# The first loads and statistics of a transformer block, in another order

## Chip, cores and metric

The kernel runs on one core of a Trainium2 chip. The metric is the device time of one execution in microseconds, the median of several runs. Before the change it is 292.81 us, the median of 3 runs (292.77 to 293.06).

## What is computed

A block with attention and an MLP over 2048 tokens of 640 features, bf16 in and out. Cut to what matters here:

```python
x = A_x                                           # 1 x 2048 x 640
h = x + attention(layernorm(x), wq, wk, wv, wo)   # 32 heads of 20, four segments of 512 tokens,
                                                  # causal softmax in a segment, linear memory between segments
out = h + silu(layernorm(h) @ w1) @ w2            # 640 -> 1728 -> 640

def layernorm(x):
    m, v = mean(x), var(x)                        # over the 640 features
    return (x - m) / sqrt(v + 1e-5)
```

The first segment's attention needs the normalized tokens of blocks 0 to 3 (128 tokens each), transposed so that features lie on partitions, and the weights wq, wk, wv (640 x 640, 800 KB each).

## The kernel before

The program is a list of named tasks. Each task issues a few instructions on one engine, and each engine runs its own instructions in the order in which the tasks stand in a hand-written list, `ORDER` (from line 382). No planner moves anything: a task that waits holds up everything behind it on its engine. In the list, a digit after the colon is the buffer or PSUM bank that the task takes, and a letter after a slash picks the engine where there is a choice (A is ScalarE, D is VectorE, G is GpSimd). `Tracker` (line 45) works out the semaphore waits from what each instruction reads and writes. One rule in it matters below: PSUM banks are one region each, and a read of PSUM by any engine other than TensorE is booked as if it were a write (lines 81 to 84), so that a later writer of the bank waits for that reader.

The work around the change is the beginning of the first segment. For token block b the tasks are:

- `x0`, `x1`, `x2`: loads of block 0, block 1, blocks 2 and 3 (line 595), all on SyncE's queue. Behind them on SyncE, in the list's order: the query weights in two pieces (`w_q0`, `w_q1`), the key weights in two pieces (`w_k0`, `w_k1`), the value weights (`w_wv`), `beta`, and then `x4` and `x8`, the tokens of blocks 4 to 11, which wait for the first key piece.
- `n1_stb`: mean and variance of block b. On VectorE that is two bn_stats, a bn_aggr, and for the blocks called early an addition of eps (lines 784 to 793). On ScalarE it is two activations over the 640 features that accumulate, the mean and then the squares (lines 778 and 780). Blocks 0, 1, 3 are on VectorE and block 2 on ScalarE; for that one a small task `n1_mnb` on ScalarE gives the mean in its final scale (line 801).
- `n1_rsb`: the power -1/2 on GpSimd; one instruction for early blocks (line 808), two for the others (lines 811 and 813).
- `n1_apb`: subtract the mean, multiply by the result, on VectorE (line 819).
- `n1_tpb`: five 128 x 128 transposes on TensorE as matmuls with the identity, into a pair of PSUM banks (line 828).
- `n1_teb`: copies these out of PSUM into `tT`, on ScalarE (line 837) or VectorE (line 838).
- `pr000x`, `pr001x`, `pr001y`, `pr000y`: the first projections of queries and keys from the raw weights, in halves of two blocks (line 752). x needs blocks 0 and 1, y needs blocks 2 and 3. Each is cut into `.0` (three chunks of 128 features) and `.1` (two chunks).
- `re_wqc`, `re_wkc`: copies of the weights into the arrangement that the later projections use (lines 745 and 747).

`zpad` is a small array of zeros that VectorE clears first. TensorE begins with matmuls on it that compute nothing (`fill25`, `fill4`, `fill8`, `fill2`, by their number, lines 636 to 638); `fill4`, `fill8` and `fill2` all write PSUM bank 5. `warm` is an activation on ScalarE that fetches the table of functions ahead of its first use (line 618). In the list of before, the order on TensorE is fill25, fill4, fill8, n1_tp0, n1_tp1, fill2, n1_tp3, pr000x.0, n1_tp2, pr000x.1, pr001x, pr001y, pr000y. Block 2's transpose takes banks 4 and 5.

After these come the rest of the segment, which alternates scores, exponentials, masks and products with values, and the other segments and the MLP woven between them.

Of the kernel before, what the change touches and what calls it, by code (L numbers as in the profile page):

```python
# [11 lines left out]
PE, AC, DV, PO, SP = "pe", "act", "dve", "pool", "sp"  # L12
# [333 lines left out]
D = 640  # L346
# [26 lines left out]
KS = [range(0, 3), range(3, 5)]  # L373
# [7 lines left out]

ORDER = """
x0:0 zpad:0 iota fill25:7 vpad0 x1:3 sel halfc mq0 x2:5,6 warm:0 w_q0:0 epsc w_q1 n1_st0:1 w_k0:0 w_k1 w_wv:0 n1_st1:0
n1_rs0 beta n1_ap0:0 n1_rs1 fill4:5 n1_st2:5,1 n1_st3:4 fill8:5 mq1 n1_tp0:2 n1_ap1:2 n1_rs3 n1_te0:1 n1_tp1:0 n1_rs2
fill2:5 n1_ap3:3 n1_mn2 n1_te1 n1_tp3:6 n1_ap2 re_wq1/A:0 pr000x.0:3 n1_te3/D x4:2,10,11,1 n1_tp2:4 pr000x.1
x8:9,8,4,7 n1_te2 pr001x.0:1 qe000x/D:0 re_wk1/G pr001x.1 re_wk2/A pr001y.0:2 re_wk4/G pr001y.1 qe001x pr000y.0:6
qe001y pr000y.1 re_wk3/G pr010.0/C:0 pa001:2 qe000y ex001:1 re_wq2/G qk0a0:4,1 lsc0 pr010.1 e0a2:0 lsc1 pr011.0:7
qe010/D:0 e0a0 pr011.1 qk0b0:0,2 qe011/D pr020.0/C:6 e0b2:3 mk0a pb001 pr020.1/C re_wk0/G n1_st4:3 e0b0 qk0e0:2,4
pr021.0:7 re_wq4/G e0e0:5 n1_st5:1 v00.0:0 vpad2 n1_rs4 e0e2 v00.1 qe020/D:0 pr021.1 n1_rs5 n1_st10:7 ve00:0 qk1a0:2,4
# [94 lines left out]
def build(nc, es, A_x, A_wq, A_wk, A_wv, A_wo, A_beta, B_x, B_w1, B_w2, out):  # L484
    T = Tracker()
# [9 lines left out]
    G = Graph(pools)  # L495
# [7 lines left out]
    wv_sb = sb("wv_sb", [128, NC, D], BF16)  # L503
# [65 lines left out]
    def R(*items):  # L569
        r = []  # L570
        for a, subs in items:
            r += a.keys(subs)
        return r

    def dma(name, reads, writes, fn, prio, bw, kind="plain", lane=None, engs=(SP,)):
        ln = T.lane(name) if lane is None else lane

        def emit(eng):
            T.add(eng, lambda e: fn(e), reads=R(*reads), writes=R(*writes), lane=ln)
        cost = {"tr": 1.31, "plain": 0.47, "sb": 0.72, "fix": 0.47}[kind]  # L580
        t = G.task(name, {e: cost for e in engs}, emit, reads, writes, prio, mode=kind, bw=bw)
        return t
# [4 lines left out]
    X = [G.alloc("x") for _ in range(12)]  # L587
    W = {k: G.alloc(k) for k in ("wq", "wk", "wv", "wo", "w1", "w2")}
    C = G.alloc("const")
# [3 lines left out]
    sT0 = G.alloc("sT")  # L593

    def load_x(b0, n, prio, bw=2.1, kind="plain", engs=(SP, AC)):
        s0 = b0 % 12
        dma(f"x{b0}", [(W["wk"], ["p"])] if b0 >= 4 else [], [(X[b], [0]) for b in range(b0, b0 + n)],
            lambda e: e.dma_start(out=x_tok[:, s0:s0 + n, :], in_=xv[:, b0:b0 + n, :]), prio, bw, kind, engs=engs)

    def load_w(k, dst, src, prio, bw, wr, kind="plain", engs=(SP, AC)):  # L600
        dma("w_" + k, [(W["wk"], ["p"])] if kind == "plain" else [], wr, lambda e: e.dma_start(out=dst, in_=src), prio, bw, kind, engs=engs)

    cw = lambda w: w.rearrange("(c p) e -> p c e", p=128)
    load_x(0, 1, -100, 2.30, "fix", (SP,))
    load_x(1, 1, -99, 2.33, "fix", (SP,))
    load_w("wv", wv_sb[:, :, :], cw(A_wv), -98, 4.96, [(W["wv"], [0])], "fix", (SP,))
    load_x(2, 2, -97, 4.79, "fix", (SP,))
    dma("beta", [], [(C, ["beta_bc"])],
        lambda e: e.dma_start(out=beta_bc[:, :],
                              in_=A_beta.rearrange("(o n) -> o n", o=1).to_broadcast([128, H])), -92, 4.65, "fix")  # L610
    for w_, (n_, src) in enumerate((("q", A_wq), ("k", A_wk))):
        for z, ks in enumerate(KS):
            k0_, k1_ = ks[0], ks[-1] + 1
            load_w(f"{n_}{z}", wraw[:, w_, k0_:k1_, :], cw(src)[:, k0_:k1_, :], -94 + w_, 6.58, [(sT0, [f"{n_}{z}"])] + ([(W["wk"], ["p"])] if n_ + str(z) == "k0" else []), "fix",
                   (SP,))
    G.task("zpad", {DV: 0.3}, lambda e_: T.add(DV, lambda e: e.memset(zpad[:, :], 0.0), writes=R((C, ["zpad"]))),
           [], [(C, ["zpad"])], -101)
    G.task("warm", {AC: 1.15}, lambda e_: T.add(AC, lambda e: e.activation(
        out=w2_sb[:, NF - 1:NF + 1, :], in_=zpad[:, 0:1].unsqueeze(2).to_broadcast([128, 2, D]), func=ACT.Tanh),
        reads=R((C, ["zpad"])), writes=R((W["w2"], [4, 5]))), [(C, ["zpad"])], [(W["w2"], [4, 5])], -100)  # L620
# [28 lines left out]
    def vpad(par, vt, wr=()):  # L649
# [8 lines left out]
        writes=["iota"], prio=-70)  # L658
    cst("sel", DV, 0.12, lambda e: e.tensor_scalar(out=ident[:, :], in0=iot[:, :], scalar1=0.0, scalar2=None,
                                                   op0=ALU.is_equal), reads=["iota"], writes=["sel"], prio=-70)  # L660
    sel = ident[:, :].rearrange("p (r e) -> p r e", e=32)[:, :, 0:VS]
# [5 lines left out]
        out=bsel[:, :], in_=bsel[:, :], pattern=[[0, NG], [-32, 4]], compare_op=ALU.is_equal, fill=0.0, base=-DH,  # L667
        channel_multiplier=1), reads=["bsel"], writes=["bsel"], prio=-1)
    cst("lsc2", DV, 0.25, lambda e: e.tensor_reduce(
        out=lsc[:, :], in_=bsel[:, :].rearrange("p (g r) -> p g r", r=4), axis=mybir.AxisListType.X, op=ALU.add),  # L670
# [95 lines left out]
    def layer_norm(tag, b, xa, xsub, dstA, i, prio):  # L766
# [5 lines left out]
        def e_stats(eng):  # L772
# [17 lines left out]
            if early:  # L790
                T.add(DV, lambda e: e.tensor_scalar(out=mvt[:, s, 1:2], in0=mvt[:, s, 1:2], scalar1=EPS, scalar2=None,
                                                    op0=ALU.add),
                      reads=R((st, ["mv"])), writes=R((st, ["mv"])))
        early = tag == "n1_" and b in (0, 1, 3)
        onact = tag == "n1_" and b == 2
        G.task(f"{tag}st{b}", {AC: 1.6} if onact else {DV: 1.03}, e_stats, [(xa, xsub)],
               [(st, ["s0", "mv"] if onact else ["s0", "s1", "mv"])] + ([(xn, [0])] if onact else []), prio)
        if onact:
# [55 lines left out]
    def declare_front(s):  # L854
# [5 lines left out]
        for i in range(4):  # L860
            layer_norm("n1_", 4 * s + i, X[4 * s + i], [0], xTa, i, k0 + P["ln1"] + P["ln1s"] * i if s else -30 + i)
# [531 lines left out]
```

## Time and profile before

| | |
|---|---|
| median of the runs | 292.81 us |
| the profiled execution | 292.8 us |
| its span, first to last instruction | 291.1 us |
| TensorE busy in the span | 283.0 us (97%) |
| ScalarE busy | 224.7 us (77%) |
| VectorE busy | 208.7 us (72%) |
| GpSimd busy | 138.1 us (47%) |
| granted TensorE clock | 1.00 throughout |

Times in the trace count from the first instruction. A row of a timeline has the start, the time to the end of the last of the merged instructions, the engine, the line of the kernel, the operation, what it writes and reads, how many, and in brackets how long the engine was idle before it and what ended that. A row of the chain of waits has start, length and the piece of work. Matmuls overlap, so the time of one says less than the distance between two.

### The profile page before, as it was taken

What the parts mean: (1) busy time and instruction counts of PE and PEld (TensorE: products, weight loads), DVE (VectorE), ACT (ScalarE), POOL (GpSimd) and SP (SyncE); (2) the same over time, 40 slices, a digit from 0 to 9 for tenths busy, and PEclk for the clock granted to TensorE, in tenths of its full rate; (3) what the DMA queues carried; (4) which work ended last, traced back from release to release, by engine and by line L of the source; (5) the groups of instructions that cost most, each with busy time, mean ns of one, the idle gap of its engine ahead of it and who ended that gap; (6) DMA issues with size and microseconds to landing.
All of it is one profiled execution on the core that took longest, in us unless ns stands there. A gap on an engine that the chain in (4) does not pass through costs nothing.

```text
span 291.1 us, 10526 instructions
## 1 busy us (share of the span) xinstructions
PE 283.0 (97%) x4587; PEld 156.9 (54%) x4587; DVE 208.7 (72%) x435; ACT 224.7 (77%) x286; POOL 138.1 (47%) x275
## 2 busy tenths in 40 slices
PE   8999989999999999999999999999999999999995
PEld 6544434445544446566643554655565557754674
DVE  5599889769998679369979972776676659436513
ACT  4999999999999999999689989999849750024300
POOL 4686668608670766609516761638435531200000
PEclk9999999999999999999999999999999999999999
DMA  7916439854565333343551327512110031340004
GB/s 207 350 57 125 85 65 303 116 55 79 121 110 126 67 86 101 47 76 60 101 183 17 66 43 102 78 19 49 25 25 2 2 69 26 75 131 0 3 5 160
DMA packets 48734, 24.86 MB, mean 85 GB/s; under 512 B 38896, under 2 KB 47472, under 8 KB 48688
## 3 DMA queue, kind: packets, MB, share of 16 engines
q1 hardware_dynamic: 48688, 24.19, 37.9%
q8 instruction: 36, 0.59, 0.9%
q14 instruction: 10, 0.08, 0.1%
HBM read 10.41 MB, written 2.62 MB: 45 GB/s over the span
## 4 chain that ended last, share of the span: by engine, by line
PE 79%; ACT 13%; DVE 4%; DMA 2%; POOL 1%; issue 1%; SPq 0%; DVEq 0%; ACTq 0%
PE ps_all L565 41%; PE ps_all L566 23%; ACT PT L1024 9%; PE ps_all L1003 7%; PE ps_all L1059 5%; ACT PT L1020 2%; DMA x_tok<-in_A_x_dram 2%; PE ps_all L1130 1%; PE ps_all L752 1%; PE ps_all L1268 1%; ACT ex L930 1%; POOL PT L1036 1%; DVE om L1149 1%; ACT oTs L1073 1%; PE ps_all L1189 1%
## 5 line engine op out<-in xcount | busy, mean ns | idle before, releaser
L1024 ACT ACTIVATE PT<-ps_all 128x1024 bf16<-128x1024 f32 x122 | 117.9, 1030 | 7.9 <-PE ps_all L1003 6.8
L1036 POOL TENSOR_SCALAR_AFFINE_SELECT PT<-PT 128x512 bf16<-128x512 bf16 x128 | 81.6, 666 | 71.6 <-ACT PT L1024 59.5
L1281 ACT ACTIVATE th<-ps_all 128x512 f32<-128x512 f32 (+1 forms) x56 | 31.5, 591 | 30.1 <-PE ps_all L565 22.5
L1287 DVE SCALAR_TENSOR_TENSOR sT<-th,ps_all 128x512 bf16<-128x512 f32 (+1 forms) x56 | 36.2, 661 | 16.8 <-ACT th L1281 16.5
L1020 ACT ACTIVATE PT<-ps_all 128x2048 bf16<-128x2048 f32 x19 | 35.7, 1878 | 3.5 <-PE ps_all L1003 3.4
L565 PE MATMUL ps_all<-w_sb,sT 128*128 128x320 bf16 x252 | 37.0, 299 | 0.0
L565 PE MATMUL ps_all<-tT,w_sb 128*128 128x512 bf16 x151 | 36.4, 380 | 0.0
L1324 DVE SCALAR_TENSOR_TENSOR x_tok<-ps_all,x_tok 128x640 bf16<-128x640 f32 (+1 forms) x17 | 13.2, 782 | 24.5 <-PE ps_all L566 16.1
L565 PEld LDWEIGHTS ps_all<-w_sb,sT 128*128 128x128 bf16 x252 | 23.7, 98 | 11.0 <-issue 1.7
L566 PE MATMUL ps_all<-w_sb,sT 128*32 128x320 bf16 x784 | 28.8, 299 | 0.0
L785 DVE BATCH_NORM_STATS2 stt<-x_tok 128x6 f32<-128x320 bf16 x62 | 27.0, 478 | 2.0 <-DMA x_tok<-in_A_x_dram 1.9
L566 PE MATMUL ps_all<-tT,w_sb 128*32 128x512 bf16 x436 | 27.1, 380 | 0.0
L566 PEld LDWEIGHTS ps_all<-w_sb,sT 128*32 128x32 bf16 x784 | 20.1, 97 | 6.7 <-issue 0.9
L565 PEld LDWEIGHTS ps_all<-tT,w_sb 128*128 128x128 bf16 x151 | 13.6, 98 | 16.1 <-issue 1.9
L1111 POOL TENSOR_TENSOR otok<-otok,om 128x320 bf16<-128x320 bf16 x24 | 18.2, 781 | 4.2 <-DVE otok L1098 4.2
L565 PE MATMUL ps_all<-wv_sb,tT 128*128 128x320 bf16 x130 | 19.9, 300 | 0.2 <-DVE zf L677 0.2
L811 POOL TENSOR_TENSOR rst<-mvt,eps_c 128x1 f32<-128x1 f32 x29 | 5.8, 201 | 27.4 <-DVE mvt L788 27.4
L819 DVE TENSOR_SCALAR xn_rot<-x_tok,mvt,rst 128x640 bf16<-128x640 bf16 x32 | 16.7, 533 | 2.5 <-POOL rst L813 1.3
L813 POOL TENSOR_TENSOR rst<-rst,eps_c 128x1 f32<-128x1 f32 x29 | 16.4, 567 | 2.3
L1246 DVE TENSOR_TENSOR x_tok<-ps_all,x_tok 128x640 bf16<-128x640 f32 x16 | 13.0, 812 | 6.0 <-PE ps_all L565 6.0
L1059 PE MATMUL ps_all<-PT,Vx 128*32 128x512 bf16 (+3 forms) x384 | 16.9, 300 | 0.2 <-ACT PT L1024 0.2
L1098 DVE TENSOR_TENSOR otok<-ps_all,rd 128x320 bf16<-128x320 f32 x32 | 15.7, 491 | 1.1
(116 smaller groups left out, 427.8 us busy)
## 6 DMA issues: line engine op xcount, KB each, us to landing
out_dram<-x_tok SPq DMA_DIRECT2D x15, 160.0 KB, 2.0
w_sb<-in_B_w_dram SPq DMA_DIRECT2D x5, 432.0 KB, 4.6
x_tok<-in_A_x_dram SPq DMA_DIRECT2D x3, 640.0 KB, 5.1
w_sb<-in_B_w_dram SPq DMA_DIRECT2D x3, 480.0 KB, 4.1
QKV<-QK SPq DMA_DIRECT2D x12, 72.0 KB
wv_sb<-in_A_wv_dram SPq DMA_DIRECT2D x1, 800.0 KB, 8.9
wo_sb<-in_A_wo_dram SPq DMA_DIRECT2D x1, 800.0 KB, 4.8
w_sb<-in_B_w_dram SPq DMA_DIRECT2D x1, 640.0 KB, 4.7
```

The costliest lines, as they stand in the source:

```text
L565: return [lambda e: e.matmul(out, lhsT=lhsT, rhs=rhs, start=start, stop=stop)]
L566: return [lambda e, p=p: e.matmul(out[p:p + 32, :], lhsT=lhsT[:, p:p + 32], rhs=rhs, start=start, stop=stop, tile_position=(0, p)) for p i ...
L785: T.add(DV, lambda e, hh=hh: e.bn_stats(out=stt[:, s, 6 * hh:6 * hh + 6], in_=xb[:, 320 * hh:320 * hh + 320]), reads=R((xa, xsub)), writes ...
L819: T.add(eng, lambda e: e.tensor_scalar(out=xn_rot[:, xn.slot, :], in0=x_tok[:, b % 12, :], scalar1=mvt[:, s, 0:1], scalar2=rst[:, s, :], o ...
L1003: fns.append(lambda e, j=j, o=o, r=r, q0=q0, q1=q1, qa=qa, ka=ka: e.matmul(ps_all[:, o:o + q1 - q0], lhsT=ka[32 * r:32 * r + DH, 128 * j:1 ...
L1020: T.add(AC, lambda e: e.activation(out=o, in_=src, func=ACT.Exp, scale=SCALE), reads=[("ps", z.slot + q) for z in (a, b) for q in range(2) ...
L1024: T.add(AC, lambda e: e.activation(out=pt[:, pta.slot, q0:q0 + 2, 0:width], in_=sc3[:, b0:b0 + 2, 0:width], func=ACT.Exp, scale=SCALE), re ...
L1036: fns.append(lambda e, v=v: e.affine_select(out=v, in_=v, pattern=[[0, 4], [1, 128]], compare_op=ALU.is_ge, fill=0.0, base=0, channel_mult ...
L1059: fns.append(lambda e, j=j, r=r, h=h, pa=pa, pt=pt, co=co, q0=q0, ji=ji: e.matmul(bank(po)[32 * r:32 * r + 32, q0:hi], lhsT=vtile(vx)[:, j ...
L1111: T.add(PO, lambda e: e.tensor_tensor(out=o_dst, in0=o_dst, in1=m, op=ALU.add), reads=R((oma, WH), *osub), writes=R(*osub))
L1281: T.add(AC, lambda e: e.activation(out=th[:, tha.slot, lo:hi], in_=bank(ps)[:, lo:hi], func=ACT.Tanh, scale=0.5), reads=R((ps, [0])), writ ...
L1287: T.add(DV, lambda e: e.scalar_tensor_tensor(out=sT[:, f, lo:hi], in0=th[:, tha.slot, lo:hi], scalar=1.0, in1=bank(ps)[:, lo:hi], op0=ALU. ...
```

## The change

- Blocks 0 and 1 come in one load, blocks 2 and 3 in a second; both on SyncE.
- The query weights come in one load, issued by ScalarE, which waits for `zpad` to be cleared; it stands ahead of `warm` on that engine.
- The key weights come in one load on SyncE, which waits until blocks 2 and 3 have landed. `w_wv` waits for the query weights.
- Statistics: blocks 0 and 2 on VectorE with the early form, blocks 1 and 3 on ScalarE with the other form.
- In the list, the first part of segment 0 is written anew: `n1_st2` stands ahead of `n1_ap0` on VectorE, `fill8` between `n1_tp0` and `n1_tp1`, block 0's evacuation is on VectorE, blocks 1 and 2 on ScalarE, block 3 on VectorE, and `n1_tp2`, `n1_te2` and `fill2` stand ahead of `pr000x.0`.

```diff
 ORDER = """
-x0:0 zpad:0 iota fill25:7 vpad0 x1:3 sel halfc mq0 x2:5,6 warm:0 w_q0:0 epsc w_q1 n1_st0:1 w_k0:0 w_k1 w_wv:0 n1_st1:0
-n1_rs0 beta n1_ap0:0 n1_rs1 fill4:5 n1_st2:5,1 n1_st3:4 fill8:5 mq1 n1_tp0:2 n1_ap1:2 n1_rs3 n1_te0:1 n1_tp1:0 n1_rs2
-fill2:5 n1_ap3:3 n1_mn2 n1_te1 n1_tp3:6 n1_ap2 re_wq1/A:0 pr000x.0:3 n1_te3/D x4:2,10,11,1 n1_tp2:4 pr000x.1
-x8:9,8,4,7 n1_te2 pr001x.0:1 qe000x/D:0 re_wk1/G pr001x.1 re_wk2/A pr001y.0:2 re_wk4/G pr001y.1 qe001x pr000y.0:6
+x0:0,3 zpad:0 iota w_q:0 fill25:7 vpad0 sel halfc mq0 x2:5,6 warm:0 epsc w_k:0 w_wv:0 beta n1_st0:1 n1_st1:0,2 n1_rs0 n1_st2:5 fill4:5 n1_ap0:0 n1_rs1 mq1 n1_mn1 n1_tp0:2 n1_ap1 fill8:5 n1_tp1:0 n1_rs2 n1_st3:4,3 n1_ap2:1 n1_mn3 n1_rs3 n1_te0/D:1 n1_te1/A n1_tp2:4 n1_ap3 n1_te2 fill2:5 pr000x.0:3 pr000x.1 re_wq1/A:0 n1_tp3:6 n1_te3/D x4:2,10,11,1 x8:9,8,4,7 pr001x.0:1 qe000x/D:0 re_wk1/G pr001x.1 re_wk2/A pr001y.0:2 re_wk4/G pr001y.1 qe001x pr000y.0:6
...
-    load_x(0, 1, -100, 2.30, "fix", (SP,))
-    load_x(1, 1, -99, 2.33, "fix", (SP,))
-    load_w("wv", wv_sb[:, :, :], cw(A_wv), -98, 4.96, [(W["wv"], [0])], "fix", (SP,))
-    load_x(2, 2, -97, 4.79, "fix", (SP,))
+    load_x(0, 2, -100, 2.80, "fix", (SP,))
+    load_x(2, 2, -97, 3.40, "fix", (SP,))
+    dma("w_q", [(C, ["zpad"])], [(sT0, ["q0", "q1"])],
+        lambda e: e.dma_start(out=wraw[:, 0, :, :], in_=cw(A_wq)), -94, 4.3, "fix", engs=(AC,))
+    dma("w_k", [(X[2], [0])], [(sT0, ["k0", "k1"]), (W["wk"], ["p"])],
+        lambda e: e.dma_start(out=wraw[:, 1, :, :], in_=cw(A_wk)), -93, 3.8, "fix")
+    dma("w_wv", [(sT0, ["q0"])], [(W["wv"], [0])],
+        lambda e: e.dma_start(out=wv_sb[:, :, :], in_=cw(A_wv)), -92, 4.5, "fix")
...
-        early = tag == "n1_" and b in (0, 1, 3)
-        onact = tag == "n1_" and b == 2
+        early = tag == "n1_" and b in (0, 2)
+        onact = tag == "n1_" and b in (1, 3)
```

More of the change, by code (lines that the diff above doesn't have):

```diff
@@ L603, in build @@
     cw = lambda w: w.rearrange("(c p) e -> p c e", p=128)
-    load_x(0, 1, -100, 2.30, "fix", (SP,))
-    load_x(1, 1, -99, 2.33, "fix", (SP,))
-    load_w("wv", wv_sb[:, :, :], cw(A_wv), -98, 4.96, [(W["wv"], [0])], "fix", (SP,))
-    load_x(2, 2, -97, 4.79, "fix", (SP,))
+    G.task("zpad", {DV: 0.3}, lambda e_: T.add(DV, lambda e: e.memset(zpad[:, :], 0.0), writes=R((C, ["zpad"]))),
+           [], [(C, ["zpad"])], -101)
+    load_x(0, 2, -100, 2.80, "fix", (SP,))
[6 more added lines that the diff above has]
+        lambda e: e.dma_start(out=wv_sb[:, :, :], in_=cw(A_wv)), -92, 4.5, "fix")
     dma("beta", [], [(C, ["beta_bc"])],
@@ L610, in build @@
                               in_=A_beta.rearrange("(o n) -> o n", o=1).to_broadcast([128, H])), -92, 4.65, "fix")
[L611 to L617, printed above, removed]
     G.task("warm", {AC: 1.15}, lambda e_: T.add(AC, lambda e: e.activation(
```

## The prediction

> **What bounds the kernel now.** I read the page first, then the chain of waits in order of time, then the busy time by stretches.
>
> ```profile
> span 291.1 us, 10526 instructions
> PE 283.0 (97%) x4587; PEld 156.9 (54%) x4587; DVE 208.7 (72%) x435; ACT 224.7 (77%) x286; POOL 138.1 (47%) x275
> ...
> PE 79%; ACT 13%; DVE 4%; DMA 2%; POOL 1%; issue 1%; SPq 0%; DVEq 0%; ACTq 0%
> ```
>
> TensorE is busy for 97% of the span, and the chain that ended last is 92% TensorE and ScalarE. Transfers hold 2% of it, and that 2% is one piece at the very start:
>
> ```profile
> 1.72 4.91 DMA x_tok<-in_A_x_dram
> ...
> 9.35 0.45 PE ps_all L828 x5
> 9.80 0.47 PE ps_all L752 x12
> ...
> 10.31 0.45 PE ps_all L828 x5
> 10.77 2.07 PE ps_all L752 x68
> ```
>
> Blocks 2 and 3 land at 1.72 + 4.91 = 6.63. I call that moment T. Statistics, rstd, normalization and the transposes (line 828) follow. The first projection (line 752, task pr000x.0) starts at 9.76; I call that S, so S = T + 3.13. After S the chain is engine work to the end, and both engines on it are full:
>
> ```profile
> 13.90:40.00 26.10, 24.56 (x309) 11.76 (x307) 23.10 (x53) 26.02 (x31) 19.16 (x41) 1.00 0.45 97
> 40.00:100.00 60.00, 58.92 (x1034) 27.87 (x1030) 51.77 (x110) 58.47 (x69) 33.53 (x72) 1.00 0.59 120
> ```
>
> The columns after the length are TensorE, weight loads, VectorE, ScalarE, GpSimd, granted clock, transfer share and GB/s. From 13.9 to 40, ScalarE is busy 26.02 of 26.10 us. Nothing there can take up a late start, so a shift of S arrives at the end whole. The change edits only what lies before S; the question is how far S moves.
>
> **The change part by part.** *Transfers.* In the trace of before:
>
> ```profile
> 0.80 1.35 SPq L598 DMA_DIRECT2D x_tok<-in_A_x_dram  x3
> 0.90 0.17 DVE L616 MEMSET zpad<- 128x128 uint32 x1 [0.90 <-PEq L1378]
> 2.20 1.00 SPq L601 DMA_DIRECT2D sT<-in_A_wq_dram  x2
> 10.17 0.92 SPq L598 DMA_DIRECT2D x_tok<-in_A_x_dram  x2
> ...
> x_tok<-in_A_x_dram SPq DMA_DIRECT2D x2, 160.0 KB, 2.3
> x_tok<-in_A_x_dram SPq DMA_DIRECT2D x1, 320.0 KB, 4.9
> ...
> 3.00:3.80 0.80, 0.80 (x6) 0.59 (x4) 0.70 (x2) 0.36 (x1) 0.00 (x0) 1.00 0.86 136
> 3.80:6.60 2.80, 2.80 (x18) 2.06 (x17) 2.06 (x8) 0.00 (x0) 1.44 (x4) 1.00 1.01 339
> ```
>
> Three token issues of 0.45 us become two, so the issue for blocks 2 and 3 starts at 1.26 instead of 1.72, with the same 640 KB of tokens on SyncE. New is the query load of 800 KB on ScalarE's queue, issued once VectorE has cleared zpad, at about 1.1; before, no weight issue starts ahead of 2.20, behind the tokens on the same queue. No row shows two queues loading at once, so I bound the new T. Low: the second token load now ends where block 1 did, 1.26 + 2.3 = 3.5, and 320 KB more at 339 GB/s take 1.0: 4.5. High: as many query bytes as token bytes are moved ahead, 640 KB at 339 GB/s, 1.9 us more than now: 8.6. I take the nearest row, today's 6.6: 0.46 earlier by issue, later by what the queries take.
>
> By the Trainium skill, page "DMA: Bandwidth & Descriptors", section "Queues, rings and completion order", SyncE and ScalarE each own one row of rings on the same 16 engines, and each engine takes turns between rows. By that rule the sum would lie toward the high end; it is the first rival.
>
> *Statistics and normalization.* Block 1 goes from VectorE to ScalarE, 2 from ScalarE to VectorE, 3 from VectorE to ScalarE. What counts is the order: VectorE now has block 0's statistics, block 2's statistics, and only then block 0's normalization (n1_ap0). Before, block 0 was normalized at 5.56 and transposed under the fillers; now this waits for T. The rows of block 3 and block 1 give the durations:
>
> ```profile
> 5.56 0.44 DVE L819 TENSOR_SCALAR xn_rot<-x_tok,mvt,rst 128x640 bf16<-128x640 bf16 x1
> 6.65 0.89 DVE L785 BATCH_NORM_STATS2 stt<-x_tok 128x6 f32<-128x320 bf16 x2 [0.66 <-DMA x_tok<-in_A_x_dram]
> 7.89 0.44 DVE L819 TENSOR_SCALAR xn_rot<-x_tok,mvt,rst 128x640 bf16<-128x640 bf16 x1
> ...
> 8.38 0.45 PE L828 MATMUL ps_all<-ident,xn_rot 128*128 128x128 bf16 x5 [0.36 <-DVE xn_rot L819]
> 8.67 0.38 PE L637 MATMUL ps_all<-zpad 128*128 128x256 bf16 x2
> ...
> L637 PE MATMUL ps_all<-zpad x16: 272/273/318, 6.0 to 8.8; 128*128 128x256 bf16 x16
> ```
>
> From landing to the start of the next normalization VectorE takes 7.89 - 6.63 = 1.26; the normalization ends 0.44 later, T + 1.70; the transpose starts at 8.38 - 8.33 = 0.05 behind it, T + 1.75, and gives TensorE free 8.67 - 8.38 = 0.29 later, T + 2.04.
>
> *Eight fillers moved.* Task fill8 now stands between the transposes of blocks 0 and 1. Two fillers took 0.38 and one lasts 0.273, so each further one costs 0.11. Eight are 0.88: block 1's transpose starts at T + 2.92 and ends 0.45 later, T + 3.37. Block 1's normalization (T + 2.1) is ready by then.
>
> *The two evacuations on ScalarE and the last filler.*
>
> ```profile
> 9.02 0.69 ACT L837 ACTIVATE tT<-ps_all 128x640 bf16<-128x640 f32 x1
> 9.60 0.73 ACT L745 ACTIVATE wqr<-sT 128x640 bf16<-128x640 bf16 x1
> 10.80 0.70 ACT L837 ACTIVATE tT<-ps_all 128x640 bf16<-128x640 f32 x1 [0.47 <-PE ps_all L828]
> ```
>
> Block 1's evacuation starts 0.04 after its transpose (10.31 + 0.45 = 10.76 to 10.80) and takes 0.69: T + 4.10. Block 2's, next on ScalarE, may start 0.11 before that end (9.60 against 9.71) and takes 0.70: T + 4.69. Now comes what the diff doesn't say: block 2's transpose holds PSUM banks 4 and 5, task fill2 writes bank 5, and in the new order it stands behind block 2's evacuation and ahead of pr000x.0. The tracker books a PSUM read by another engine as exclusive, so fill2 waits until ScalarE has emptied the bank, and all of TensorE's stream waits behind these two matmuls of zeros. Before, fill2 ran at 8.67, ahead of that transpose. With 0.05 for the hand-over (9.71 to 9.76) and 2 x 0.11, S = T + 4.96, against T + 3.13: **+1.83**.
>
> *Behind S.* Block 2's transpose is done and block 3's lies inside instead. The pair of projections for blocks 2 and 3 (pr001y.0) then waits for block 3's evacuation, which is on VectorE:
>
> ```profile
> 10.17 0.82 DVE L838 CAST tT<-ps_all 128x640 bf16<-128x640 f32 x1
> 10.70 2.14 PE L752 MATMUL ps_all<-tT,sT 128*32 128x256 bf16 x68
> ```
>
> Four of these matmuls run side by side: 17 groups in 2.14 less a tail of 0.27 give 0.11 a group. Five groups of pr000x end at S + 0.55, the transpose starts at S + 0.59 and ends at S + 1.04, the evacuation at S + 1.04 + 0.04 + 0.82 = S + 1.90, pr001y.0 starts at S + 1.95. Before, it started at 11.50 + 0.05 = S + 1.79: **+0.16**.
>
> *What is covered.* ScalarE's statistics need about 1.8 us each (two passes over 640 elements instead of VectorE's four short instructions). Block 1's runs after the warm-up activation:
>
> ```profile
> 0.80 1.28 ACT L618 ACT_TABLE_LOAD   x1 [0.80 <-PEq L1378]
> 2.09 1.27 ACT L618 ACTIVATE w_sb<-zpad 128x1280 bf16<-128x1280 bf16 x1
> 6.65 0.74 ACT L778 ACTIVATE xn_rot<-x_tok 128x640 bf16<-128x640 bf16 x1 [3.29 <-DMA x_tok<-in_A_x_dram]
> ...
> 8.25 0.19 ACT L780 ACTIVATION_READ_ACCUMULATOR xn_rot<-x_tok,stt 128x1 f32 x1
> ```
>
> If the query issue goes ahead of the table load, warm-up ends near 1.1 + 0.5 + 1.28 + 1.27 = 4.2 and block 1's statistics at 6.0, under the wait for T = 6.6. Block 3's end at T + 1.8, and te1 comes at T + 3.4. This cover goes when T falls below 4.6: then 4.2 + 2 x 1.8 + the evacuations hold S near 9.5 whatever lands. Key weights now wait for T on SyncE, with value weights, beta and the loads of blocks 4 to 11 queued behind that wait. Their 800 KB need 2.3 + 1.9 (640 KB more than a 160 KB load, at 339 GB/s), so they are in at T + 4.3 = 10.9; the first use is pr001x at about S + 0.9 = T + 5.9.
>
> ```profile
> 4.29 0.48 SPq L601 DMA_DIRECT2D wv_sb<-in_A_wv_dram  x1
> 11.20 2.10 POOL L747 COPY wkr<-sT 128x640 bf16<-128x640 bf16 x5 [1.50 <-DMA sT<-in_A_wk_dram]
> 13.69 0.22 ACT L664 ACTIVATE bsel<-beta_bc 128x32 f32<-128x32 bf16 x1
> 16.72 0.87 DVE L785 BATCH_NORM_STATS2 stt<-x_tok 128x6 f32<-128x320 bf16 x2
> ...
> wv_sb<-in_A_wv_dram SPq DMA_DIRECT2D x1, 800.0 KB, 8.9
> ```
>
> Value weights follow (2.4 us at 339 GB/s) and are in near 13.3, as now (4.29 + 8.9); beta comes with them, and its reader moves from 13.69 to 15.7. The two loads of blocks 4 to 11 are issued near 10.9 instead of 10.17, while their first reader, at 16.72, comes 2 us later. GpSimd's rearrangement of key weights waited for the keys until 11.20, S + 1.4; it would now start about S - 0.7. I cost all of these at nothing. If a cover is gone, each costs what the load is late.
>
> **Sum.** T at today's value, 0.0 + 1.83 + 0.16 = +2.0 on the profiled execution's 292.8 (span 291.1 and 1.7 around it), which is also the median: **294.8**.
>
> **The rivals.** (1) *The query load takes every second turn*: T = 8.6, 292.8 + 2.0 + 2.0 = 296.8. For it: 1.01 of the engines' time is already used from 3.80 to 6.60, so another stream can only take from the tokens. Against: the query issue starts later than the first token issue, and the earlier token issue pays 0.46 back. (2) *The tokens land early*: T near 4.5. For it: the stretch at 136 GB/s, in which blocks 2 and 3 were slow to begin, need not come back. Then 4.5 - 6.6 + 2.0 gives 292.7, no change. (3) *Faster*: the tokens run on at the best rate and the table load is not pushed back. Then T = 3.9, S = 8.9, and the end is 0.7 earlier: 292.1. It decides only from T below 4.0; against it stands that 655 KB must then move by about 3.5, which takes 385 GB/s from 1.8 on, over the 339 of the row, with the query load beside it. (4) *TensorE slows down in the new idle stretch.* The fillers show a fast and a slow pace at a granted clock of 1.00:
>
> ```profile
> 1.12 6.62 PE L637 MATMUL ps_all<-zpad 128*128 128x256 bf16 x37 [1.12 <-DVE zpad L616]
> ...
> 1.20:6.00 4.80, 4.80 (x23) 3.37 (x24) 1.00 0.81 238
> ```
>
> 23 took 0.21 each until 6.0, against 0.11 later. Now 29 of the 37 run at the start and end at about 6.7 (six more at 0.11 after 6.0), and TensorE idles until T + 1.75 = 8.4. If the slow pace comes back, fill8 costs 0.8 more, fill2 and block 1's transpose 0.2 each, and the 20 groups of the first projections up to 2.0: 298.0. Against it, the trace has gaps of 0.3 us only, so it says nothing on 1.7 us.
>
> The Trainium skill, page "TensorE: Matmul & The Clock Gate", section "Part 1: The HAM clock gate (the "warmup" mystery)", puts the fall-back after an idle window of about 3.4 us. By that rule an idle of 1.7 us keeps the fast pace, and a T near 8.6 would be at the edge.
>
> **How the numbers follow.** About 0.2%, 0.6 us, is what a measurement of this kernel can tell from no change. Forecast (T from 5.2 to 7.9, 293.4 to 296.1): 0.64. Rival 1: 0.12. Rival 2: 0.12. Rival 3: 0.05. Rival 4: 0.07. Faster is rival 3, 0.05; same is rival 2, 0.12; the rest is slower, 0.83. The range goes from the low bound of T, 292.7, to the high one, 296.8.
>
> **What would show it.** In the changed profile: block 0's normalization (line 819) behind two sets of statistics, about 1.3 us after the landing of blocks 2 and 3; eight fillers between the first two transposes; two fillers directly before the first line 752, begun just after ScalarE's second evacuation; S about 5.0 after T. If fill2 does not wait, S is T + 4.1 and the time 294.0. If T is 4.5 or less, or if S comes at 9.8 or before, the forecast is wrong; if S moves by 2 and the time doesn't, then some slack behind S took it up that I did not see.

## The result, and the profile after

The changed kernel takes **297.52 us**, the median of four runs (297.04 to 297.81), against 292.79 for the kernel before: ratio 1.0161, interval 1.0143 to 1.0179. It is slower, as forecast, but by 4.7 us where 2.0 were forecast, and above the range. The profiled execution took 297.55. First the head of its page, the row of the granted TensorE clock in tenths (40 slices of the span), and two of its transfers with their time from issue to landing:

```profile
span 295.8 us, 10522 instructions
...
PE 285.7 (97%) x4587; PEld 158.1 (53%) x4587; DVE 207.9 (70%) x432; ACT 226.2 (76%) x290; POOL 138.5 (47%) x276
...
PEclk9689999999999999999999999999999999999999
...
sT<-in_A_wq_dram ACTq DMA_DIRECT2D x1, 800.0 KB, 6.0
sT<-in_A_wk_dram SPq DMA_DIRECT2D x1, 800.0 KB, 4.8
```

The clock row was full throughout before; now the second and third slice stand at 6 and 8 tenths. The timeline shows where the start of the kernel went (lines after the change are three or four lower than before):

```profile
1.10 0.43 ACTq L606 DMA_DIRECT2D sT<-in_A_wq_dram  x1
1.12 5.82 PE L633 MATMUL ps_all<-zpad 128*128 128x256 bf16 x29 [1.12 <-DVE zpad L601]
1.56 1.28 ACT L614 ACT_TABLE_LOAD   x1 [1.56 <-DVE zpad L601]
...
7.24 0.37 SPq L608 DMA_DIRECT2D sT<-in_A_wk_dram  x1
...
8.48 0.80 DVE L815 TENSOR_SCALAR xn_rot<-x_tok,mvt,rst 128x640 bf16<-128x640 bf16 x2
...
8.98 0.45 PE L824 MATMUL ps_all<-ident,xn_rot 128*128 128x128 bf16 x5 [2.04 <-DVE xn_rot L815]
...
9.27 1.55 PE L633 MATMUL ps_all<-zpad 128*128 128x256 bf16 x8
...
10.61 1.27 PE L824 MATMUL ps_all<-ident,xn_rot 128*128 128x128 bf16 x10
...
12.74 0.61 PE L633 MATMUL ps_all<-zpad 128*128 128x256 bf16 x2 [0.86 <-ACT tT L833]
...
13.28 1.26 PE L748 MATMUL ps_all<-tT,sT 128*32 128x256 bf16 x20
...
14.47 0.71 PE L824 MATMUL ps_all<-ident,xn_rot 128*128 128x128 bf16 x5
...
15.11 2.46 PE L748 MATMUL ps_all<-tT,sT 128*32 128x256 bf16 x60
...
18.60 1.03 ACT L1020 ACTIVATE PT<-ps_all 128x1024 bf16<-128x1024 f32 x1
```

Two rows of the chain of waits belong to it, the token load and the two evacuations on ScalarE:

```profile
1.32 5.90 DMA x_tok<-in_A_x_dram
...
11.38 1.31 ACT tT L833 x2
```

T, the landing of blocks 2 and 3, is 1.32 + 5.90 = 7.22. S, the first line of the first projection, is 13.28 = T + 6.06. I call the start of the first exponential E: 18.60 = S + 5.32. Before, the three were 6.63, 9.76 and 13.86. So E is 4.74 later, and the span is 4.7 longer: from E to the end it is 277.2 in both profiles. The whole loss lies ahead of E.

The order is the one that the forecast drew: block 0's normalization 1.26 behind T (8.48), eight fillers between the first two transposes, two fillers begun 0.05 behind ScalarE's second evacuation, with TensorE idle 0.86 before them. What the forecast had given a chance of 0.07 is there too. Stretches of the same profile, with TensorE, weight loads, VectorE, ScalarE, GpSimd, granted clock, transfer share and GB/s behind the length:

```profile
6.23:9.64 3.41, 1.37 (x15) 1.02 (x14) 2.17 (x7) 1.84 (x5) 1.96 (x8) 1.00 0.30 63
9.64:13.05 3.41, 2.55 (x19) 1.80 (x16) 1.33 (x3) 1.67 (x3) 1.63 (x3) 0.50 1.06 381
13.05:16.47 3.42, 3.42 (x55) 1.99 (x57) 1.16 (x2) 0.93 (x3) 2.26 (x7) 0.50 1.03 333
16.47:20.00 3.53, 3.53 (x63) 1.77 (x55) 0.99 (x2) 3.09 (x7) 0.26 (x1) 1.00 0.28 99
```

From 9.64 to 16.47, two stretches of 3.41 us, TensorE had half its clock. It begins after a stretch in which TensorE was idle 2.04 in one piece (6.94 to 8.98) and busy 1.37 of 3.41. Between 9.75 and 10.39 the fillers start 0.21 apart. So did the first fillers of the kernel, which go from 0.21 apart to 0.11 near 6.23, one stretch of 3.41 ahead of 9.64: they ran at the same half pace, though the profile gives a clock of 1.00 for them.

The last difference is in the transfers. Packets, MB and share of the 16 engines by queue (q1 is SyncE's, q10 ScalarE's), from 3.4 to 4.5:

```profile
q10 hardware_dynamic: 333, 0.43, 104.4%
q1 hardware_dynamic: 6, 0.00, 1.1%
```

and from 4.6 to 6.5:

```profile
q1 hardware_dynamic: 267, 0.32, 48.5%
q10 hardware_dynamic: 253, 0.31, 47.0%
```

For 1.1 us the query weights had the engines alone, while the load of blocks 2 and 3, issued at 1.32, stood; then the two shared them.

### The profile page after: what moved, and what is told of

Its sections match the earlier page's. It is cut to its first block, busy times and chain, and to the rows that moved or that the text cites. A ratio compares the mean times of both kernels' runs of the same rounds, so it can differ in the third digit from the quotient of the medians.

```text
span 295.8 us, 10522 instructions
## 1 busy us (share of the span) xinstructions
PE 285.7 (97%) x4587; PEld 158.1 (53%) x4587; DVE 207.9 (70%) x432; ACT 226.2 (76%) x290; POOL 138.5 (47%) x276
## 4 chain that ended last, share of the span: by engine, by line
PE 82%; ACT 10%; DVE 4%; DMA 2%; POOL 1%; issue 1%; SPq 0%; ACTq 0%
PE ps_all L562 42%; PE ps_all L563 23%; PE ps_all L999 7%; ACT PT L1020 6%; PE ps_all L1055 5%; DMA x_tok<-in_A_x_dram 2%; ACT PT L1016 2%; PE ps_all L748 1%; PE ps_all L1185 1%; PE ps_all L1126 1%; PE ps_all L1264 1%; PE ps_all L633 1%; POOL PT L1032 1%; DVE om L1145 1%; PE ps_all L824 1%; ACT oTs L1069 1%
## 5 line engine op out<-in xcount | busy, mean ns | idle before, releaser
L781 DVE BATCH_NORM_STATS2 stt<-x_tok 128x6 f32<-128x320 bf16 x60 | 26.2, 478 | 4.2 <-DMA x_tok<-in_A_x_dram 4.0
L809 POOL TENSOR_TENSOR rst<-rst,eps_c 128x1 f32<-128x1 f32 x30 | 17.0, 568 | 2.3
```

What stands on the lines that cost most here:

```text
L781: T.add(DV, lambda e, hh=hh: e.bn_stats(out=stt[:, s, 6 * hh:6 * hh + 6], in_=xb[:, 320 * hh:320 * hh + 320]), reads=R((xa, xsub)), writes ...
L809: T.add(PO, lambda e: e.tensor_tensor(out=rst[:, s, :], in0=rst[:, s, :], in1=eps_c[:, 1:2], op=ALU.pow), reads=R((st, ["r"]), (C, ["half" ...
```

## The experiments

Theory A says that the forecast's steps hold, and that the half clock adds about 2 us to them because TensorE is idle too long. Theory B says that the clock is a side effect and costs little, and that late loads and the order make the whole loss. The first group tells these apart. The second splits loads from order, and the third looks for single steps and for a version that is faster. The task list is shown with one task to a line. Medians in one table, then T, S and E of each profile; ratios are to the runs of the kernel before on the same chip, with their interval. The medians of these runs of before were 292.63 (for e1 to e4), 292.74 (e5 to e7, f1) and 292.56 (e8, e9, c1, f2):

| kernel | median us | ratio | T | S | E | span |
|---|---|---|---|---|---|---|
| before | 292.79 | | 6.63 | 9.76 | 13.86 | 291.1 |
| after | 297.52 | 1.0161 (1.0143 to 1.0179) | 7.22 | 13.28 | 18.60 | 295.8 |
| e7_fill14 | 295.73 | 1.0091 (1.0056 to 1.0127) | 7.10 | 12.17 | 16.50 | 294.1 |
| e1_fill | 296.18 | 1.0128 (1.0103 to 1.0152) | 7.12 | 12.62 | 16.95 | 295.5 |
| e2_fill2 | 294.95 | 1.0076 (1.0048 to 1.0104) | 7.12 | 11.32 | 15.75 | 293.7 |
| e3_both | 295.54 | 1.0099 (1.0084 to 1.0114) | 7.09 | 11.29 | 15.72 | 293.9 |
| e8_fill8 | 294.76 | 1.0088 (1.0064 to 1.0112) | 7.14 | 11.42 | 15.76 | 292.8 |
| e9_ap0 | 295.14 | 1.0098 (1.0065 to 1.0131) | 6.98 | 11.28 | 15.61 | 292.8 |
| e4_loads | 294.68 | 1.0079 (1.0054 to 1.0104) | 7.11 | 10.24 | 14.87 | 293.1 |
| e5_order | 294.58 | 1.0057 (1.0041 to 1.0073) | 5.29 | 10.49 | 14.83 | 291.7 |
| e6_qsp | 293.80 | 1.0036 (1.0020 to 1.0052) | 4.80 | 10.27 | 15.01 | 292.0 |
| c1_nofill | 292.65 | 1.0005 (0.9993 to 1.0018) | 5.89 | 9.02 | 13.11 | 291.0 |
| f1_tokens2q | 293.43 | 1.0020 (1.0005 to 1.0035) | 4.88 | 9.66 | 14.08 | 291.2 |
| f2_tokens2q | 292.83 | 1.0013 (1.0002 to 1.0023) | 4.93 | 10.06 | 13.46 | 290.8 |

**More fillers under the wait for T.** Ten more (e7_fill14, as shown), and 21 more (e1_fill, with `fill25:5` at the same place). They write zeros to a bank that nobody reads.

```diff
 n1_st2:5
-fill4:5
+fill14:5
 n1_ap0:0
```

> The changed kernel with 10 more fillers ahead of block 0's transpose instead of 21, so that they end before it is ready. Theory A: no overrun as with 21, clock 1.00, first projection at T + 5.0 = 12.1, first exponential near 16.4, time 295.4. Theory B: 297.5.

> One edit on the changed kernel: 21 more matmuls of zeros ahead of block 0's transpose, so that TensorE does not idle from 6.9 to 9.0. Nothing else moves. Theory A (the pace of TensorE): the idle stretch makes the granted clock fall to 0.50 from 9.64 to 16.47, and that costs about 2.2 of the 4.7 us. Then the clock stays 1.00 here, the first projection starts at T + 5.0 = 12.2, and the time is near 295.3. Theory B (loads and order alone): the slow pace is only a by-product of waiting, and the time stays at 297.5 within 0.4.

The timeline of e7_fill14, and two of its stretches of 3.41 us. They are counted from 4.77, where in this execution the first fillers go from 0.21 apart to 0.11, as they do near 6.23 in the kernel after:

```profile
8.85 0.45 PE L824 MATMUL ps_all<-ident,xn_rot 128*128 128x128 bf16 x5 [1.53 <-DVE xn_rot L815]
...
9.14 1.04 PE L633 MATMUL ps_all<-zpad 128*128 128x256 bf16 x8
...
10.01 0.72 PE L824 MATMUL ps_all<-ident,xn_rot 128*128 128x128 bf16 x10
...
10.49 1.30 ACT L833 ACTIVATE tT<-ps_all 128x640 bf16<-128x640 f32 x2 [1.50 <-PE ps_all L824]
11.85 0.39 PE L633 MATMUL ps_all<-zpad 128*128 128x256 bf16 x2 [1.11 <-ACT tT L833]
...
12.17 0.73 PE L748 MATMUL ps_all<-tT,sT 128*32 128x256 bf16 x20
12.83 0.45 PE L824 MATMUL ps_all<-ident,xn_rot 128*128 128x128 bf16 x5
...
16.50 1.02 ACT L1020 ACTIVATE PT<-ps_all 128x1024 bf16<-128x1024 f32 x1
```

```profile
4.77:8.18 3.41, 2.55 (x23) 2.04 (x21) 1.39 (x6) 2.10 (x7) 1.89 (x7) 1.00 0.50 167
8.18:11.59 3.41, 1.89 (x23) 1.62 (x23) 2.47 (x7) 1.91 (x5) 1.56 (x3) 1.00 0.90 286
```

With 1.53 idle instead of 2.04, and stretches busy 2.55 and 1.89 instead of 1.37, the clock stays at 1.00, in the profile and in all four runs. Everything else of the order is as in the kernel after, so the rows can be laid beside each other. The eight fillers need 10.01 - 9.14 = 0.87 against 10.61 - 9.27 = 1.34; from block 1's transpose to the first evacuation 10.49 - 10.01 = 0.48 against 11.38 - 10.61 = 0.77; the two fillers before S 0.32 against 0.54; the first 20 projections 0.66 against 1.19. S is T + 5.07 instead of T + 6.06, and E is S + 4.33 instead of S + 5.32: the half clock costs 0.99 ahead of S and 0.99 behind it. The medians differ by 1.79. This speaks for A: the order's steps, as the forecast had them, plus some 2 us for the clock.

In e1_fill the clock holds as well, but its fillers run past T:

```profile
1.13 8.35 PE ps_all L633 x50
```

In this execution they hold block 0's transpose until 9.31, T + 2.19 instead of T + 1.75, and E is 0.45 later than in e7_fill14: a filler that overruns the wait is paid for. The median is 0.45 above that of e7_fill14 too, and 0.9 above the 295.3 that was expected. How far the fillers run is no constant of the list: in e3_both below, the same 50 leave block 0's transpose at 8.85, T + 1.76.

**The last two fillers ahead of block 2's transpose** (e2_fill2), and this with e1_fill's change (e3_both).

```diff
 n1_tp1:0
+fill2:5
 n1_rs2
...
 n1_te2
-fill2:5
 pr000x.0:3
```

> One edit on the changed kernel: the two fillers ahead of the first projection go in front of block 2's transpose, so that they no longer wait for ScalarE to empty bank 5. Theory A: the first projection starts right behind block 1's evacuation, at 12.1 instead of 13.3; TensorE is then at work for nearly all of 9.64 to 13.05, the clock returns at 13.05 instead of 16.47, and the time is near 295.4. Theory B: only the bank wait goes, 0.7 to 1.2 us, and the time is 296.3 to 296.8 with the clock low until 16.5.

> Both edits, 21 more fillers and the two fillers ahead of block 2's transpose. Theory A: clock 1.00, first projection at T + 4.15 = 11.4, time 292.8 + 0.6 (T) + 1.0 + 0.2 = 294.6. Theory B: like the edit of the bank wait alone, 296.3 to 296.8.

The timeline of e2_fill2:

```profile
8.88 0.45 PE L824 MATMUL ps_all<-ident,xn_rot 128*128 128x128 bf16 x5 [1.68 <-DVE xn_rot L815]
...
11.32 0.73 PE L748 MATMUL ps_all<-tT,sT 128*32 128x256 bf16 x20 [0.34 <-issue]
...
15.75 1.02 ACT L1020 ACTIVATE PT<-ps_all 128x1024 bf16<-128x1024 f32 x1
```

Its stretch with the long idle piece, counted from where its fillers change pace:

```profile
6.76:10.17 3.41, 1.73 (x20) 1.34 (x19) 2.79 (x8) 1.84 (x5) 2.04 (x7) 1.00 0.50 122
```

S is T + 4.20; the prediction had said T + 4.1 for a fill2 that does not wait. Against e7_fill14, in which the clock holds too, two matmuls of zeros cost 5.07 - 4.20 = 0.87 by their wait for bank 5 (predicted: 4.96 - 4.1), and 0.75 in E; the medians differ by 0.78. In e2_fill2 TensorE idled 1.68 and the clock held in the profile; in one of its four runs, the slowest at 295.73, the mean granted clock was 0.994, as for one stretch of 3.41 us at half. Theory A had expected it to fall here as in the kernel after, since up to block 1's transpose the two lists are the same. So the same start of the list loses the clock in one execution and keeps it in another: four of four runs lost it there, one of four here.

e3_both came out at 295.54 where 294.6 was expected. Its S and E are those of e2_fill2; what is longer lies behind E (278.2 to the end against 277.9), and most of the difference of the medians isn't in these profiles. One piece shows, far behind the edits:

```profile
120.05 1.25 PE L562 MATMUL ps_all<-tT,w_sb 128*128 128x512 bf16 x5 [0.45 <-issue]
```

TensorE stands 0.45 there and the profile names nothing that it waits for; before, the same work follows without a gap. The rest of the miss I can't place. More fillers bring nothing where the clock holds without them.

**The loads alone** (e4_loads): the order and the statistics of before with the loads of after.

```diff
-x0:0 zpad:0 iota fill25:7 vpad0 x1:3 sel halfc mq0 x2:5,6 warm:0 w_q0:0 epsc w_q1 n1_st0:1 w_k0:0 w_k1 w_wv:0
+x0:0,3 zpad:0 iota w_q:0 fill25:7 vpad0 sel halfc mq0 x2:5,6 warm:0 epsc n1_st0:1 w_k:0 w_wv:0
...
```

> The loads of the changed kernel with the order and the statistics of the one before. Theory A: blocks 2 and 3 land at T = 7.2 as in the changed kernel, the fillers stand where they stood, the clock holds, and the first projection starts at T + 3.1 = 10.3; the key weights land at 12.0 and are wanted at 11.3, 0.7 late; 292.8 + 0.6 + 0.7 = 294.1. Theory B: the loads carry most of the loss, and the time is 296 or more. If neither the loads nor the keys matter, 293.4 or less.

The chain of waits, and below it a row of the table of waits from 8 to 16 (total, times, longest):

```profile
7.13 4.84 DMA sT<-in_A_wk_dram
...
12.02 1.82 PE ps_all L751 x60
```

```profile
PEld ps_all L751 <- DMA sT<-in_A_wk_dram: 0.7, 1, 0.7
```

S is 10.24 = T + 3.13, exactly the old distance. Then TensorE waits 0.7 for the key weights, which land at 11.97, 4.8 behind the wait for T. E is 1.0 later than before: 0.5 because T is later, and 0.5 of this wait. The median is 2.05 above before, though, and expected were 294.1; the profile's other 1.0 lies behind E (278.2 against 277.2). It comes in single steps far from the edits: counted from E, the exponentials are 0.3 late from 51.6 on, 0.5 from 70.7 and 0.9 from 173.5. What makes these steps stays open, so the loads alone are shown to cost the 1.0 ahead of E and no more. One of the four runs, the slowest at 295.94, has a mean clock of 0.994.

**The order and the statistics alone** (e5_order): the loads of before with the list of after.

```diff
-x0:0,3 zpad:0 iota w_q:0 fill25:7 vpad0 sel halfc mq0 x2:5,6 warm:0 epsc w_k:0 w_wv:0 beta n1_st0:1
+x0:0 zpad:0 iota fill25:7 vpad0 x1:3 sel halfc mq0 x2:5,6 warm:0 w_q0:0 epsc w_q1 w_k0:0 w_k1 w_wv:0 beta n1_st0:1
...
```

> The order and the statistics of the changed kernel with the loads of the one before (tokens in three loads, all weights on SyncE without a wait). Theory A: T = 6.6 as before, the first projection at T + 5.0 = 11.6 if the clock holds, first exponential about 2.0 us later than before, time 294.7; TensorE idles from 6.9 to 8.4 only, so in most runs the clock should hold, and where it falls the time is 296 to 297. Theory B (loads carry the loss): 293.4 or less.

Its timeline, with the statistics of block 2 that begin 0.03 behind T, and below it a row of the chain of waits:

```profile
5.32 0.89 DVE L782 BATCH_NORM_STATS2 stt<-x_tok 128x6 f32<-128x320 bf16 x2 [1.03 <-DMA x_tok<-in_A_x_dram]
...
10.49 0.73 PE L749 MATMUL ps_all<-tT,sT 128*32 128x256 bf16 x20
...
14.83 2.97 ACT L1021 ACTIVATE PT<-ps_all 128x1024 bf16<-128x1024 f32 x3
```

```profile
1.13 6.22 PE ps_all L634 x29
```

The median, 294.58, is 1.84 above before; 1.99 had been forecast for an unmoved T. The profile doesn't have that T: the same issues on the same queue that landed at 6.63 in the profile before have landed by 5.3 here. So T is no constant of the loads. The profiled execution is the fastest of its ten (293.57), and T in the other nine is not known. Nor does T hold the first transpose here: the 29 fillers do, until 7.19 (T + 1.90). S comes at T + 5.20, and E, at S + 4.34, is 1.0 later than before with a T that is 1.3 earlier. The order alone costs time, then; that the median is near the forecast doesn't confirm its sum.

**The query weights on SyncE, behind the tokens** (e6_qsp).

```diff
-        ..., -94, 4.3, "fix", engs=(AC,))
+        ..., -94, 4.3, "fix")
...
 x2:5,6
+w_q:0
 warm:0
```

> One edit on the changed kernel: the query load moves to SyncE's queue, behind the token loads. Theory Q (ScalarE's queue takes the engines from blocks 2 and 3): blocks 2 and 3 land at 4.6 to 5.5 instead of 7.2, the idle stretch before the first transpose goes, the clock holds, the first projection starts near 10.3, and the time is 293.0 to 293.6. Rival (a second load on one queue begins slowly by itself, as in the kernel before): T stays at 6.5 or more and the time at 295 or more.

The timeline (the issue of the key weights waits for T), and a row of the chain of waits:

```profile
4.82 0.37 SPq L608 DMA_DIRECT2D sT<-in_A_wk_dram  x1
...
9.95 0.39 PE L633 MATMUL ps_all<-zpad 128*128 128x256 bf16 x2 [0.83 <-ACT tT L833]
...
14.87 0.23 ACT L660 ACTIVATE bsel<-beta_bc 128x32 f32<-128x32 bf16 x1 [0.34 <-DMA beta_bc<-in_A_beta_dram]
```

```profile
9.16 5.69 DMA beta_bc<-in_A_beta_dram
```

With the same token loads at the same times, T is 4.8; with the query weights on ScalarE's queue it was 7.0 to 7.2 in all eight profiles that have them there. So the query load, on that queue and issued ahead of the second token load, is what holds blocks 2 and 3 back; here it is behind them both on the queue and in time, so this run doesn't separate the two. E doesn't come 2.3 earlier than in e7_fill14, only 1.5: 0.4 goes ahead of S, which is T + 5.47, and 0.4 to beta. Beta, issued behind key and value weights that wait in turn, lands at 14.85, and its reader stands right ahead of the first exponential. What the forecast had named as the cover of beta is gone when T falls. The median of 293.80 is just above the 293.0 to 293.6 that were expected.

**Eight fillers back ahead of block 0's transpose** (e8_fill8), and **block 0's normalization back ahead of block 2's statistics** (e9_ap0).

```diff
 mq1
 n1_mn1
+fill8:5
 n1_tp0:2
 n1_ap1
-fill8:5
 n1_tp1:0
```

```diff
 n1_rs0
+n1_ap0:0
 n1_st2:5
 fill4:5
-n1_ap0:0
 n1_rs1
```

> One edit on the changed kernel: the eight fillers go back ahead of block 0's transpose. Theory A: they no longer stand between the two transposes, TensorE works until 7.8 and idles 1.1 us instead of 2.0, the clock holds, block 1's evacuation follows its own transpose, and the first projection starts at T + 4.2 = 11.3 (still behind the bank wait); first exponential near 15.8, time 294.9. Theory B: 297.5, or 296.6 if only the fillers' own 0.9 us goes.

> One edit on the changed kernel: VectorE normalizes block 0 ahead of block 2's statistics. Theory A: block 0's transpose and the eight fillers run by 7.9, before block 1's normalization; the clock holds; block 1's transpose at about 9.0, first projection at T + 4.2 = 11.3, first exponential near 15.8, time 294.9. Theory B: 297.5.

S is T + 4.28 and T + 4.30. The eight fillers between the transposes cost 5.07 - 4.28 = 0.79 (predicted: 0.88). Block 0's normalization, put back, takes the first transpose and the fillers out of the wait (they end at 7.9) but then block 2's normalization waits for GpSimd's rstd until 9.2, and S gains no more than 0.77. Each of the three repairs of the order gives about 0.8 by itself, of the 1.94 by which S - T in e7_fill14 is over the old 3.13. Medians of 294.76 and 295.14 against 294.9 for both are near. In e8_fill8 TensorE idled 1.60, not the expected 1.1, and one of its four runs shows 0.994. The four runs of e9_ap0 show the price of the clock inside one kernel: 294.34 and 294.67 at 1.00, 295.61 at a mean of 0.994, 297.03 at 0.988. With 0.006 x 294 x 2 = 3.5 us at half for the first and twice that for the second, each such stretch costs 1.1 to 1.3. The single runs at 0.994 of e2_fill2, e4_loads, e8_fill8 and c1_nofill below are 1.2 to 1.45 above the median of their kernel's other runs. Only in the kernel after does the second stretch add little: its runs at 0.994 take 297.04 and 297.5, those at 0.988 take 297.55 and 297.81.

**The kernel before without 12 of its fillers** (c1_nofill).

```diff
 n1_rs1
-fill4:5
 n1_st2:5,1
 n1_st3:4
-fill8:5
 mq1
```

> The kernel before with 12 of its 39 matmuls of zeros left out (those of fill4 and fill8), and no other edit; no useful work goes or moves. Theory A: TensorE then idles about 1.7 us in two pieces between 6.6 and 9.3, as in the changed kernel, the granted clock falls to 0.50 in some or all runs, and those take 2 us more: 294 to 295. Theory B (the pace is only a by-product): 292.7 within 0.4, since these matmuls compute nothing.

The longest idle piece of TensorE ahead of S, in the timeline:

```profile
7.64 0.45 PE L828 MATMUL ps_all<-ident,xn_rot 128*128 128x128 bf16 x5 [0.70 <-DVE xn_rot L819]
```

The time is the same, 292.65, so theory A's 294 to 295 was a miss. T was 5.9 here, and the longest idle piece 0.7: the removal did not make the idle that it was meant to make. One of ten runs, the slowest (293.85), shows 0.994. The run doesn't say how short an idle piece can bring the clock down.

**Tokens on both queues, weights behind them** (f1_tokens2q, f2_tokens2q), to see whether the change's parts can be put together better: blocks 2 and 3 as ScalarE's first issue, the weights on SyncE without waits, fill8 and fill2 left out, four fillers behind block 1's transpose, block 0 evacuated early; f2_tokens2q also has block 3's transpose ahead of the first projection.

```diff
-    load_x(2, 2, -97, 3.40, "fix", (SP,))
+    load_x(2, 2, -97, 3.40, "fix", (AC,))
-    dma("w_q", [(C, ["zpad"])], [(sT0, ["q0", "q1"])],
+    dma("w_q", [], [(sT0, ["q0", "q1"])],
...
```

The second differs from the first by:

```diff
...
-n1_te2 pr000x.0:3 pr000x.1 re_wq1/A:0 n1_tp3:6 n1_te3/D
+n1_tp3:6 n1_te2 n1_te3/D pr000x.0:3 pr000x.1 re_wq1/A:0
...
```

> A repaired version: blocks 2 and 3 are ScalarE's first issue, at the same moment as blocks 0 and 1 on SyncE; query, key and value weights follow on SyncE without waits; statistics as in the changed kernel; block 0's transpose and the fillers stand so that no filler waits for a PSUM bank. Theory Q: the two token loads share the engines, all four blocks are in by 4.5, query weights by 7, key weights by 9.5; first projection near 8.9, first exponential 0.4 to 0.8 us earlier than before, time 292.0 to 292.4. Rival: the two queues do not run side by side, blocks 2 and 3 land at 6 or later, and the time is 293 or more.

> The repaired version with block 3's transpose ahead of the first projection instead of behind it. In the repaired version the pair of projections for blocks 2 and 3 waited for block 3's evacuation until 11.8; here that evacuation ends near 11.0. First exponential near 13.4 instead of 14.1, and the time 292.4 to 292.7, at or a little below the kernel before; if block 3's evacuation is not what held it, 293.4 as without the edit.

The timeline of f2_tokens2q:

```profile
10.06 2.37 PE L748 MATMUL ps_all<-tT,sT 128*32 128x256 bf16 x80
...
13.46 4.81 ACT L1020 ACTIVATE PT<-ps_all 128x1024 bf16<-128x1024 f32 x5
```

The first version missed what was expected of it (292.0 to 292.4): S came at 9.66 instead of 8.9, and the median is 293.43. With T at 4.9 and one unbroken run of 80 projections, f2_tokens2q has E 0.4 earlier than the profile before. Its median is 292.83 against 292.56 for before on the same chip, so it is not faster. Though all four blocks are in by 4.9, the first transpose starts at 7.58, as before: blocks 0 and 1 land later than block 0 did (VectorE's statistics begin at 4.63 instead of 3.10), and the statistics of block 2 stand ahead of block 0's normalization, which begins at 7.09. No version of these beat the kernel before.

## Why the prediction was right and wrong

**The sign and the order were right.** With the clock held, the forecast's steps come out as drawn: S = T + 5.07 for T + 4.96, E = S + 4.33 for S + 4.26 (the 4.10 of before and 0.16), in e7_fill14. The wait of fill2 for bank 5, the eight fillers between the transposes and the covered statistics on ScalarE are there with 0.87, 0.79 and nothing; the table load went behind the query issue (1.56), which left block 1's statistics under the wait for T, as foreseen. e5_order, the order without the loads, is +1.84 for +1.99 in the median; its profile has another T and another wait, so this is no proof of the sum.

**The step that failed is the fourth rival.** The sum had no term for TensorE's pace. The prediction said that the slow pace might come back in the new idle stretch, gave the time, 298.0, and then a chance of 0.07, because "the trace has gaps of 0.3 us only, so it says nothing on 1.7 us". It said nothing, and I took that for a reason against. The range, 292.7 to 296.8, was drawn over T alone and left the rival's own time out. I had also read the two paces of the fillers as two paces "at a granted clock of 1.00"; the 0.21 of the slow one is the pace at 0.50, as the fillers behind 9.64 show, so TensorE's low clock was in the trace before. The slow pace came back in all four runs of the kernel after: mean clocks of 0.988, 0.994, 0.988 and 0.994, which is two stretches or one of 3.41 us at half. It costs 1.98 in E between the two profiles, 1.79 between the medians. The parts I had priced are right in kind: the eight fillers +0.47 (for +0.8), fill2 and the transpose +0.22 and +0.29 (for 0.2 each), the work from S to E +0.99 (for up to 2.0).

The idle piece was longer than forecast, 2.04 for 1.7, because T was later. The Trainium skill, page "TensorE: Matmul & The Clock Gate", section "Part 1: The HAM clock gate (the "warmup" mystery)", has the clock fall after an idle window of about 3.4 us, in free-running windows. The trace agrees on the size and grid (9.64 to 16.47 is twice 3.41) and on the half, but not on how much idling it takes: 2.04 us of idle, in a stretch with TensorE busy 1.37 of 3.41, was enough. And a stretch busy 2.55 of 3.41 did not bring it back; the next one, busy throughout, did.

**T was mis-sized by 0.6.** The forecast took the 6.6 of the one profile before; it was 7.22, inside the bounds of 4.5 and 8.6. The mechanism is close to the first rival's, at a third of its price: ScalarE's queue took the engines from blocks 2 and 3, first alone and then by halves. The Trainium skill, page "DMA: Bandwidth & Descriptors", section "Queues, rings and completion order", has each engine take turns between the queues. The trace shows turns from about 4.6 on (267 packets to 253), but not from 3.4 to 4.5 (6 to 333); whether the second token load, issued at 1.32, had packets ready by then it doesn't show. In e6_qsp the tokens were early, at 4.8, as the second rival had it, but the end was not at 292.7: fill2 and beta held it, at 293.80. T + 3.13 for the old order held in e4_loads to the hundredth.

**The key weights were costed at nothing, and that was right only by luck.** They land at T + 4.8, not T + 4.3. In the kernel after their first reader comes at 15.11, so nothing waits; with the old order (e4_loads) they are 0.7 late. The cover named in the prediction, pr001x at T + 5.9, was itself made of the delays.

**A shift of S arrives whole**: right. From E to the end it is 277.2 in the profiles before and after, and 276.9 to 278.5 in all the others, with no relation to E. The four of the chip of e1 to e4 are at the long end (277.9 to 278.5), though the kernel before was no slower on it.

The account of the forecast's miss, in the profiles: 0.59 for T, 0.99 for the clock ahead of S, 0.99 for it behind S, and 0.18 for the small errors of the steps, together 2.75 for E (18.60 against 13.86 + 1.99 = 15.85).

What stays open: the loads alone cost 2.05 in the medians, of which the profile shows 1.0 ahead of E; and what makes the stretch behind E differ by up to 1.7 between profiles. Some of it comes in single steps, such as the 0.45 in e3_both.

## What to carry to other kernels

An idle stretch of the busiest engine that the trace before doesn't have is a term of the sum and no footnote: price the slow clock for it, and give it a chance that fits its length against the longest gap that the trace has shown to be harmless. Add up the idle pieces that lie close together, too: by the rows of e9_ap0, one long piece is not the only way to a stretch with little work (argued here, not tested). A landing time read from one execution is a draw, not a constant; here the same loads gave 5.3, 5.9 and 6.6. Matmuls that compute nothing still take their turn on the engine and wait for their bank: where a list is written anew, each of them needs a place at which its bank is long free.

## What the hardware showed that I had not expected

TensorE's clock fell to 0.50 after 2.04 us of idling, and in the profiled executions of much the same start it did not after 1.53, 1.60 and 1.68. One kernel can show both: one of four runs of e2_fill2, of e4_loads and of e8_fill8 is at 0.994, one of ten of c1_nofill, and e9_ap0 goes from 1.00 to 0.988. The longest idle pieces ahead of S in the profiles of c1_nofill, e9_ap0 and e4_loads are 0.70, 0.81 and 0.92, so a short longest piece in one profile promises nothing for the next execution. The runs of these kernels that lost the clock were not profiled; how long TensorE idled in them, and where their slow stretch lies, is not known.

Where the stretches of 3.41 begin isn't tied to the kernel. The 29 fillers, whose pace doubles at one of these borders, took 5.82 in the kernel after, 6.07 in e2_fill2 and 5.33 in e6_qsp. Counted from its own border, the stretch ahead of the fall in the kernel after was busy 1.37 of 3.41; 1.73 in e2_fill2 and 1.89 in e7_fill14 kept the clock. By this the share of work in a stretch would decide, and the place of the border with it: in e9_ap0 the 3.41 us from 7.55 on have TensorE busy only 1.29, but the borders of the profiled execution, 5.91 and 9.32, part them into stretches of 2.48 and 2.24, and the clock held. This fits the numbers, with one profiled fall among them, and was not tested by itself.

The other way the border counts as well: in e5_order TensorE began its fillers at 1.13 and was busy 2.53 of the 3.41 us up to 3.66, but the fast pace came only at 7.07, behind a stretch that was busy throughout.

Two queues with loads waiting didn't share the engines for 1.1 us: ScalarE's query load, issued 0.2 before SyncE's second token load, ran alone. Loads served in the order of their issue, whatever the queue, would give that. In f1_tokens2q, whose two token loads were issued at the same moment on the two queues, these shared the engines from 3 to 4 (157 packets to 136), which fits; no run here was made to tell.
